# A new written order for a fused attention and feed-forward kernel, planned with re-measured transfer times and freer PSUM banks

## The chip, the cores and the metric

The kernel runs on one core of a Trainium2 chip. The metric is the device time of one execution in microseconds (us). Engines are named as in the profile: PE (matrix multiply), PEld (its weight loads), DVE (vector), ACT (scalar), POOL (GpSimd) and SP, whose only work here is to issue the DMA transfers.

## What is computed

```python
q_pool = q.reshape(B, H, S // 2, 2, D).mean(axis=3)          # B 4, H 8, S 1152, D 64
scores = np.matmul(q_pool, k.transpose(0, 1, 3, 2)) / np.sqrt(D)
scores = scores - np.max(scores, axis=-1, keepdims=True)
attn = np.exp(scores)
attn = attn / (np.sum(attn, axis=-1, keepdims=True) + 1e-09)
x = np.matmul(attn, v)        # then heads side by side: 2304 tokens x 512
h = x @ w_in                  # 512 x 2048
g = np.maximum(0.01 * h, h)
out = g @ w_out               # 2048 x 512
```

The two weight matrices come as 64-bit floats, everything else as 32-bit floats.

## The kernel before

There are 32 heads and then a feed-forward part of nine blocks of 256 tokens (`NB`), which begins as soon as the heads of a batch are finished, so that heads and blocks share the engines for most of the time.

**One head** (`hd`) is a chain of steps. Each step is a small function: `load_k`, `load_q`, `load_v` issue transfers; `k_tr` and `q_tr` transpose on PE, `k_hi`, `k_lo`, `q_hi`, `q_lo` split the results into a high and a low part on ACT and DVE; `q_dup` copies the parts to the other 64 partitions by DMA; six `qk` steps on PE (L453, L456) make scores only for their row maxima, which `vmax` takes on DVE (L468) and `vneg` combines; `m_tr`, `m_cp` and `m_dma` (L488) bring the maxima into rows; nine `qkt` steps (L503) make the scores again, transposed and with the maxima subtracted, `exp` (L507) takes the exponential on ACT, `esum` (L517) adds the tiles on POOL, `pv` (L529) multiplies with v. Then comes the tail of the head: `r_mm` (L540, L545) sums over partitions, `r_cp` copies to SBUF on ACT, `r_fold` (L563) issues four tiny transfers (two from head 12 on), `r_inv` (L568, L569) takes the reciprocal on DVE, `r_row` and `r_wide` send it to DRAM and back to 64 partitions, `norm` copies the pv result out of PSUM, `scale` (L583) multiplies on POOL, and `x_out` (L589) writes the head to DRAM.

**The weights** go through `w_load`, `w_f32` (ACT, then two DVE steps L614 and L617 that build 32-bit floats from the bits), `w_hi`, `w_lo` (L629, POOL) and `w_out_dma`. In the feed-forward part `l1` (L682) multiplies with w_in, and `l2` (L814 to L816) or `l2s` (L773) with w_out.

**The order.** All instructions of an engine are issued in the order in which the program writes them, and an instruction that waits holds up everything behind it on its engine; SP's transfers are such a queue too. The order is the string `ORDER`: one letter for each of 3557 steps, the letter names the family and the steps of a family come in a fixed sequence. `Scheduler.run` goes through it. For each step it looks up when its inputs and its buffer will be free in a model of the engines, and picks by it the buffer, the PSUM banks and, where a step may run on two engines, the engine. So the model's numbers do not change the letters, but they decide slots and engines. The letters themselves were found by a search with the same model outside of the kernel. In the model a transfer step of `n` DMAs takes 0.5 us of SP for each, and lands 1.2 us after its bytes have passed at 300 KB/us:

```python
if s.lat:                                                     # Scheduler.start
    end = self.dma = max(self.dma, end + 0.45) + s.lat
    end += 1.2
```

A DVE step marked `lock` waits in the model until POOL is free, and POOL waits until such a step has ended (`at`).

**PSUM** has eight banks. The two pairs (0, 1) and (2, 3) hold the score tiles of `qkt` (kind `s`) and the pairs (4, 5) and (6, 7) hold the tiles of `k_tr`, `q_tr`, `qk` and `m_tr` (kind `tp`); `r_mm` uses bank 6 (kind `t`) and `pv` bank 7 (kind `o`).

Of the kernel before, what the change touches and what calls it, by code (L numbers as in the profile page):

```python
# [24 lines left out]
LAT = 0.12  # L25
PELAT = 0.28
# [19 lines left out]
    "!#$%()!*+,,+#$++%-,,.--().*++.,,-.-.@-BB(A-../.01-.)!!*+A,-.23C+,-3-.4433-44.3.4./(#350$A143%B4#-33$B.%24-3434"  # L46
    ".&&&-.344-)3A*554555.+B,+3(3CB,6CC-4C4C.AA6-5553../7408123!!3)DDDE44EF-.6BB*++EF(&,9GG,:6F-.384-334.G-5-343.A-"
    ".../443;4#3$%031-B7A9.-H-.443-4.55!2.33-4.)34-43.*4.++5535(/<)0,,D=31#6>$D:;7A%CEEB4-6.4A-.9555!C2?B8<34=3-43("
    ".-3443H.-.&3-434*43../++#55$>,:,3F&F6%40157G9D#E$A;D%6-4)?38GD.H4H-.3:4-2343-.4-33..-5555434.3<.*/(=>!E+,+,B?6"
# [26 lines left out]
    "STV_`V_UVVUVVVVUUUUbVVVVVVa^bb^^V`VVVV_aUVVUUVbVVVVV_``daacbccbccUb^^VVVV^UbUVVVVV__^bUUVVV`^VVVccUVUVc_abVVV^"
    "_VV_`ab``a__aV^UUVVVVVVUUVVVb`a^UUUVVVVdddVVVVVVUUVV_bUb`abb`a^^ccVVVbbc_cb`a_``aa^_VVVVVVb^__`UUb`bVaV`VVVacc"
    "cV^ba_`abbbbbbbbbbbbbcdcccccdccbbcddd"
# [991 lines left out]
```

## Time and profile before

| | |
|---|---|
| median of 3 runs | 935.74 us (935.18 to 937.49) |
| the profiled execution, its own time | 939.89 us |
| its span, first to last instruction | 938.1 us |
| PE busy | 877.3 us, 94% of the span |
| DVE, POOL, ACT busy | 519.5, 485.3, 402.5 us |
| mean granted TensorE clock | 0.974 |

The profile comes from one execution. The busy time of an engine is the union of its instructions; idle time before an instruction is put down to what released it last. A busy PE can be at either level of its clock, which the rows show beside the busy time (1.00 is 2.4 GHz, 0.50 is 1.2 GHz). "SPq" rows are DMA issues on SP: their length is the time SP spent on issuing, not the transfer.

### The profile page before, as it was taken

How to read it: one execution, taken by the hardware profiler on the slowest of the kernel's cores; microseconds unless marked ns; L12 is line 12 of the kernel's file. 1: busy time of each engine (PE TensorE's matmuls, PEld its weight loads, DVE VectorE, ACT ScalarE, POOL GpSimd, SP SyncE). 2: the span in 40 equal slices, each digit the busy share in tenths (PEclk: the TensorE clock that was granted, in tenths of full speed). 3: DMA queues.
4: the chain of work that ended last, by engine and by line, in shares of the span. 5: the costliest groups of instructions: out<-in, count | busy, mean ns of one | idle time of the engine just before them, and what ended most of it. 6: DMA issues, size and time to landing. Idle time of an engine off the chain costs nothing.

```text
span 938.1 us, 19689 instructions
## 1 busy us (share of the span) xinstructions
PE 877.3 (94%) x7736; PEld 704.5 (75%) x7736; DVE 519.5 (55%) x806; ACT 402.5 (43%) x727; POOL 485.3 (52%) x386
## 2 busy tenths in 40 slices
PE   4989878889897999999999999999999999999997
PEld 2766546566685878777777776777779999999997
DVE  6677756656676763244446154444419974553353
ACT  2655455544455434433444534533442433422231
POOL 1656555558765769476757956955582101112000
PEclk9999998998898999999999999999999999999999
DMA  5565456466667555435545465264338777467651
GB/s 153 179 185 140 152 170 186 122 182 188 192 208 259 189 165 193 126 109 148 187 125 166 118 202 152 56 178 159 118 95 257 237 220 259 161 223 232 196 180 46
DMA packets 107309, 159.74 MB, mean 170 GB/s; under 512 B 25856, under 2 KB 74304, under 8 KB 107216
## 3 DMA queue, kind: packets, MB, share of 16 engines
q1 hardware_dynamic: 107216, 158.48, 54.8%
q8 instruction: 61, 1.00, 0.4%
q14 instruction: 32, 0.26, 0.1%
HBM read 131.12 MB, written 17.90 MB: 159 GB/s over the span
## 4 chain that ended last, share of the span: by engine, by line
PE 72%; DMA 9%; DVE 7%; SPq 4%; issue 2%; POOL 2%; ACT 2%; DVEq 0%; ACTq 0%; POOLq 0%
PE banks L682 21%; PE banks L503 13%; PE banks L529 12%; PE banks L773 10%; PE banks L453 4%; PE banks L814 3%; DVE stat L468 3%; PE banks L816 2%; PE banks L815 2%; DVE raw L614 2%; DMA rt<-rs 1%; DMA kn<-in_k_dram 1%; PE banks L540 1%; SPq L563 1%; DMA rs<-rd 1%
## 5 line engine op out<-in xcount | busy, mean ns | idle before, releaser
L468 DVE TENSOR_REDUCE stat<-banks 128x1 f32<-128x1024 f32 (+3 forms) x224 | 218.8, 1007 | 144.9 <-PE banks L453 118.6
L507 ACT ACTIVATE e<-banks 128x576 f32<-128x576 f32 x232 | 147.2, 649 | 127.1 <-PE banks L503 113.9
L517 POOL TENSOR_TENSOR sm<-sm,e 128x576 f32<-128x576 f32 x116 | 164.2, 1435 | 9.7 <-ACT e L507 8.5
L682 PE MATMUL banks<-xb,ws 128*128 128x256 f32 x1152 | 156.9, 290 | 0.4 <-issue 0.4
L682 PEld LDWEIGHTS banks<-xb,ws 128*128 128x128 f32 x1152 | 146.4, 193 | 10.3 <-issue 6.9
L503 PE MATMUL banks<-qh,ka 64*128 64x288 f32 x1152 | 147.3, 330 | 2.5 <-ACT e L507 1.2
L529 PE MATMUL banks<-e,vv 128*64 128x288 f32 x928 | 137.8, 411 | 1.2 <-DVE ql L424 1.1
L503 PEld LDWEIGHTS banks<-qh,ka 64*128 64x128 f32 x1152 | 103.0, 198 | 36.1 <-issue 13.2
L453 PE MATMUL banks<-ka,qh 64*128 64x512 f32 (+1 forms) x320 | 81.7, 486 | 33.3 <-DVE stat L468 15.7
L529 PEld LDWEIGHTS banks<-e,vv 128*64 128x64 f32 x928 | 69.4, 136 | 49.7 <-issue 5.4
L503 PE MATMUL banks<-mt,hot 64*128 64x288 f32 x576 | 92.6, 303 | 3.7 <-DMA mt<-ms 3.6
L503 PE MATMUL banks<-ql,ka 64*128 64x288 f32 x576 | 91.7, 304 | 0.0
L583 POOL TENSOR_TENSOR x<-x,rs 128x288 f32<-128x288 f32 x32 | 26.4, 827 | 101.9 <-DMA rs<-rd 88.5
L453 PEld LDWEIGHTS banks<-ka,qh 64*128 64x128 f32 (+1 forms) x320 | 33.6, 195 | 58.0 <-DVE stat L468 19.6
L682 PE MATMUL banks<-ka,ws 128*128 128x256 f32 x576 | 72.5, 282 | 1.4 <-DMA ws<-wd 1.4
L682 PEld LDWEIGHTS banks<-ka,ws 128*128 128x128 f32 x576 | 70.3, 188 | 2.5 <-issue 1.8
L517 POOL TENSOR_TENSOR sm<-e 128x576 f32<-128x576 f32 x32 | 47.1, 1473 | 35.4 <-ACT e L507 30.4
L503 PEld LDWEIGHTS banks<-mt,hot 64*128 64x128 f32 x576 | 60.7, 196 | 4.8 <-DMA mt<-ms 4.8
L773 PE MATMUL banks<-wo,gg 128*128 128x256 f32 x360 | 62.6, 282 | 0.3 <-DVE gg L749 0.3
L403 POOL TENSOR_TENSOR qs<-qn 112x384 f32<-112x384 f32 x32 | 33.2, 1036 | 52.5 <-DMA qn<-in_q_dram 33.9
L503 PEld LDWEIGHTS banks<-ql,ka 64*128 64x128 f32 x576 | 60.1, 196 | 0.0
L695 POOL TENSOR_TENSOR gg<-g,gg 128x512 fp32r<-128x512 f32 x32 | 41.7, 1305 | 26.3 <-ACT gg L248 15.9
(201 smaller groups left out, 1445.3 us busy)
## 6 DMA issues: line engine op xcount, KB each, us to landing
ws<-wd SPq DMA_DIRECT2D x144, 512.0 KB
kn<-in_k_dram SPq DMA_DIRECT2D x32, 288.0 KB
qn<-in_q_dram SPq DMA_DIRECT2D x128, 72.0 KB
vv<-in_v_dram SPq DMA_DIRECT2D x32, 288.0 KB
raw<-in_moe_w_in_dram SPq DMA_DIRECT2D x16, 512.0 KB
raw<-in_moe_w_out_dram SPq DMA_DIRECT2D x16, 512.0 KB
wd<-ws SPq DMA_DIRECT2D x16, 512.0 KB
rs<-rd SPq DMA_DIRECT2D x64, 72.0 KB
```

The costliest lines, as they stand in the source:

```text
L403: ENG[e].tensor_tensor(out=qs[hd][:n], in0=a, in1=b, op=ALU.add)
L453: nc.tensor.matmul(p[:n, x, :KW], lhsT=qh[hd][r, o:o + n], rhs=kh[r, :KW], start=True, stop=True)
L468: nc.vector.tensor_reduce(out=d, in_=p, axis=AX.X, op=ALU.max)
L503: nc.tensor.matmul(p[:, x, :HW], lhsT=w[r], rhs=m[r, hf * HW:(hf + 1) * HW], start=(n == 0), stop=(n == 3))
L507: nc.scalar.activation(out=ex[hd, u], in_=sps.pop((hd, u))[:, :, :HW], func=AF.Exp)
L517: ENG[e].tensor_tensor(out=o, in0=a, in1=b, op=ALU.add)
L529: nc.tensor.matmul(p[64 * hf:64 * hf + 64, :HW], lhsT=vv[hd][:, t, :], rhs=probs(hd, t, hf), start=(t == 0), stop=(t == KT - 1),)
L583: ENG[e].tensor_tensor(out=x1s[hd], in0=x1s[hd], in1=rss.pop(hd), op=ALU.mult)
L682: nc.tensor.matmul(p, lhsT=wst[i, f][:, a, c, :], rhs=xx[i][x][:, c, :], start=(n == 0), stop=(n == 3 * KC - 1))
L695: ENG[e].tensor_tensor(out=t[:, 1], in0=gf.pop((i, fp)), in1=f32(t[:, 0]), op=ALU.subtract)
L773: nc.tensor.matmul(o, lhsT=g[i, p][:, a], rhs=w[:, x], start=(p == 0 and n == 0 and half == 0), stop=(p == FH - 1 and n == 2), skip_group_ ...
L814: nc.tensor.matmul(p, lhsT=gh, rhs=wo[f][:, 0], start=(f == hf * FH), stop=False)
```

## The change

The change replaces the string `ORDER`. It also gives the model of `Scheduler` other numbers for transfers and a limit of ten transfers under way (`FLIGHTS`), and lets three kinds of PSUM tiles lie in more banks. No step, shape or instruction form is added or removed. The diff, with the string cut to one of its lines:

```diff
+FLIGHTS = 10
 ORDER = (
-    "!#$%()!*+,,+#$++%-,,.--().*++.,,-.-.@-BB(A-../.01-.)!!*+A,-.23C+,-3-.4433-44.3.4./(#350$A143%B4#-33$B.%24-3434"
...
+    "()*+,++!+,,,!@B(B)#$--%#$.-..*--..-.+.!+,B/0(%)1A-*+,.+B-!.-CCCC2.,3A-34,--.4.34#3../&&3$40A453-(1#%-..B4A3$53"
...
     def at(self, s, e, t):
         t = max(t, self.free[e])
+        if s.lat:
+            n, each = s.lat[0], s.eng["SP"] / s.lat[0]
+            for j in range(n):
+                i = len(self.flights) + j - FLIGHTS
+                t = max(t, self.flights[i] - j * each) if 0 <= i < len(self.flights) else t
+            return t
...
         if s.lat:
-            end = self.dma = max(self.dma, end + 0.45) + s.lat
-            end += 1.2
+            end = self.dma = max(self.dma, end + 0.6) + s.lat[1]
+            end += 0.45
+            self.flights += [end] * s.lat[0]
...
-    tags["tp"] = [(None, 0, slots("bank", (4, 5), (6, 7)))]
-    tags["t"] = [(None, 0, slots("bank", (6,)))]
-    tags["o"] = [(None, 0, slots("bank", (7,)))]
+    tags["tp"] = [(None, 0, slots("bank", (4, 5), (6, 7), (0, 1), (2, 3)))]
+    tags["t"] = [(None, 0, slots("bank", (6,), (7,)))]
+    tags["o"] = [(None, 0, slots("bank", (7,), (6,)))]
...
-    def sp(n, nbytes, run=512):
-        return dict(eng={"SP": 0.5 * n}, lat=nbytes / 300e3 * max(1.0, 512 / run))
+    def sp(n, nbytes, each=0.46, rate=250e3):
+        return dict(eng={"SP": each * n}, lat=(n, nbytes / rate))
```

Each transfer step gets its own `each`: 0.47 for `load_q` (rate 200e3), 0.58 for `q_dup` and `r_wide` (there 120e3), 0.78 for `m_dma`, 0.62 for `r_fold`, 0.41 for `r_row`, 0.6 for `x_out`, 0.5 for the weights, 0.36 for `ws_load`. Lines of the kernel after the change are 8 higher than before (L563 is L571).

In the program that results, 62 of the 288 `tp` tiles lie in banks 0 to 3, 39 of them in heads 0 to 13; five `pv` tiles lie in bank 6 and five `r_mm` tiles in bank 7. `norm` stands on DVE in 17 heads (before in 7), the copy of `post` in 13 of 32 (before in 8). Matmuls of the same tiling of the array follow each other in groups; PE goes from one tiling to another 265 times, before 290 times.

**SP around `r_fold` of heads 4 and 5** (`rt` is the target of `r_fold`, `mt` of `m_dma`, `rd` of `r_row`, `rs` of `r_wide`). Before:

```order
L387 DMA qn_70<-in_q_dram 48x3x128 x4
L589 DMA xd_74<-x_1286 64x288 x2
L433 DMA qh<-qh 64x288 x2
L600 DMA raw<-in_moe_w_out_dram 128x512
L433 DMA ql<-ql 64x288 x2
L563 DMA rt<-rs 48x1x6 x8
L488 DMA mt_73<-ms 1x5x128 x2
L572 DMA rd_82<-rt 96x6
```

After:

```order
L571 DMA rt<-rs 48x1x6 x4
L608 DMA raw<-in_moe_w_in_dram 128x4x128
L447 DMA vv<-in_v_dram 128x576
L366 DMA kn<-in_k_dram 128x576
L367 DMA kn<-in_k_dram 128x64
L496 DMA mt_73<-ms 1x5x128 x2
L580 DMA rd_82<-rt 96x6
L366 DMA kn<-in_k_dram 128x576
L367 DMA kn<-in_k_dram 128x64
L608 DMA raw<-in_moe_w_in_dram 128x4x128
L441 DMA ql<-ql 64x288 x2
L584 DMA rs<-rd_82 64x288 x2
```

The eight transfers of the two heads stood together, ahead of `m_dma` of head 7; now those of head 4 stand alone, and those of head 5 follow behind the last row shown.

**DVE around `r_inv` of the same heads** (`stat_66` and `stat_67` are the maxima of even and odd heads, here 8 and 7 or 9). Before:

```order
L471 TENSOR_REDUCE neg_69<-stat_67 128x5
L468 TENSOR_REDUCE stat_66<-banks 128x1 x2
L568 TENSOR_REDUCE rt<-rt 96x6
L569 RECIPROCAL rt<-rt 96x6
L568 TENSOR_REDUCE rt<-rt 96x6
L569 RECIPROCAL rt<-rt 96x6
L468 TENSOR_REDUCE stat_66<-banks 128x1
L379 TENSOR_TENSOR ka<-banks,ka 128x2x5x64
L468 TENSOR_REDUCE stat_66<-banks 128x1
```

After:

```order
L479 TENSOR_REDUCE neg_69<-stat_67 128x5
L576 TENSOR_REDUCE rt<-rt 96x6
L577 RECIPROCAL rt<-rt 96x6
L622 TENSOR_SCALAR raw<-raw 128x512 x2
L476 TENSOR_REDUCE stat_66<-banks 128x1 x3
L387 TENSOR_TENSOR ka<-banks,ka 128x2x5x64
L476 TENSOR_REDUCE stat_66<-banks 64x1
L476 TENSOR_REDUCE stat_66<-banks 128x4
L476 TENSOR_REDUCE stat_66<-banks 64x1
L479 TENSOR_REDUCE neg_68<-stat_66 128x5
L432 SCALAR_TENSOR_TENSOR ql<-banks,qh 64x288
L576 TENSOR_REDUCE rt<-rt 96x6
```

Both reciprocals stood between the second and the third maximum of head 8; now that of head 5 stands behind all maxima of head 8.

**PE at the start.** Before:

```order
L367 MATMUL banks<-ident,kn 128x64 x10
L412 MATMUL banks<-ident,qs 128x48 x6
L367 MATMUL banks<-ident,kn 128x64 x10
L453 MATMUL banks<-ka,qh 128x512 x6
L412 MATMUL banks<-ident,qs 128x48 x6
L453 MATMUL banks<-ka,qh 128x512 x2
```

After:

```order
L420 MATMUL banks<-ident,qs 128x48 x6
L375 MATMUL banks<-ident,kn 128x64 x10
L461 MATMUL banks<-ka,qh 128x512 x4
L375 MATMUL banks<-ident,kn 128x64 x10
L461 MATMUL banks<-ka,qh 128x512 x2
L420 MATMUL banks<-ident,qs 128x48 x6
```

The transposes of q come first (on SP the transfers of q stand ahead of those of k), and two `qk` steps of head 0 stand ahead of `k_tr` of head 1.

## Rows read from the trace of the kernel before

**Rows 1.** The page, busy time by engine and granted clock by fortieth.

```profile
PE 877.3 (94%) x7736; PEld 704.5 (75%) x7736; DVE 519.5 (55%) x806; ACT 402.5 (43%) x727; POOL 485.3 (52%) x386
...
PEclk9999998998898999999999999999999999999999
```

**Rows 2.** Busy time by stretch: start:end, length, engines (instructions), clock, DMA share, GB/s.

```profile
0.00:30.00 30.00, 16.26 (x117) 11.15 (x119) 19.90 (x30) 9.30 (x17) 5.40 (x14) 1.00 0.58 164
30.00:305.00 275.00, 239.73 (x2340) 171.53 (x2338) 184.35 (x231) 146.51 (x273) 169.92 (x131) 0.91 0.59 180
305.00:705.00 400.00, 396.23 (x3446) 300.30 (x3445) 179.11 (x240) 170.36 (x318) 281.89 (x216) 1.00 0.49 147
705.00:938.10 233.10, 225.04 (x1847) 221.54 (x1843) 136.13 (x308) 76.33 (x120) 28.09 (x28) 1.00 0.61 200
```

**Rows 3.** PE's waits, 30 to 305: sum in us, times, longest.

```profile
PE banks L453 <- DVE stat L468: 12.9, 6, 5.4
PE banks L453 <- DMA qh<-qh: 5.2, 4, 2.3
PE banks L453 <- DVE ka L379: 4.1, 3, 3.6
PE banks L503 <- DMA mt<-ms: 3.6, 4, 1.5
PE banks L453 <- ACT x L248: 3.3, 2, 2.3
```

**Rows 4.** All engines' waits, 30 to 305: `norm` on ACT.

```profile
ACT x L248 <- DMA xd<-x: 17.5, 6, 4.5
```

**Rows 5.** Instructions in time, DVE and PE: start, length, what, [idle before <-releaser].

```profile
139.60 0.16 DVE L568 TENSOR_REDUCE rt<-rt 96x6 f32<-96x12 f32 x1 [3.83 <-DMA rt<-rs]
...
142.83 0.79 PE L453 MATMUL banks<-ka,qh 64*128 64x512 f32 x2 [5.44 <-DVE stat L468]
```

**Rows 6.** Instructions in time, SP's issues at the same place.

```profile
134.05 5.92 SPq L563 DMA_DIRECT2D rt<-rs  x8
```

**Rows 7.** Instructions in time, DVE at 96 and DVE, POOL and PE from 285.

```profile
96.01 3.90 DVE L614 TENSOR_SCALAR raw<-raw 128x512 uint32<-128x512 uint32 x1
...
286.70 7.97 DVE L614 TENSOR_SCALAR raw<-raw 128x512 uint32<-128x512 uint32 x1 [2.90 <-ACT raw L611]
...
285.07 5.53 POOL L517 TENSOR_TENSOR sm<-sm,e 128x576 f32<-128x576 f32 x4
290.55 2.49 POOL L629 TENSOR_TENSOR ws<-raw,ws 128x512 fp32r<-128x512 f32 x2
...
295.86 0.80 PE L453 MATMUL banks<-ka,qh 64*128 64x512 f32 x2 [5.18 <-DVE stat L468]
```

**Rows 8.** Sum over the nine stretches between 63 and 302 with clock 0.50.

```profile
sum 47.60, PE 44.75 PEld 37.48 DVE 26.75 ACT 19.18 POOL 22.00; mean PE 4.97 PEld 4.16 DVE 2.97 ACT 2.13 POOL 2.44
```

**Rows 9.** Instructions in time, PE from one tiling to another.

```profile
309.12 0.40 PE L815 MATMUL banks<-wo,gg 128*128 128x512 f32 x1
309.36 0.40 PE L816 MATMUL banks<-wo,gg 128*128 128x512 f32 x1
309.69 0.27 PE L477 MATMUL banks<-ident,neg 64*128 64x64 f32 x2
```

**Rows 10.** One line's instructions, SP's issues: min/median/max ns, first and last start.

```profile
L563 SPq DMA_DIRECT2D rt<-rs x88: 501/584/1812, 55.2 to 712.4; - x88
...
L488 SPq DMA_DIRECT2D mt<-ms x64: 691/739/837, 20.9 to 684.0; - x64
```

**Rows 11.** Instructions in time at the start.

```profile
2.12 1.87 SPq L387 DMA_DIRECT2D qn<-in_q_dram  x4
...
10.92 0.79 PE L453 MATMUL banks<-ka,qh 64*128 64x512 f32 x2 [2.65 <-DVE ka L379]
```

**Rows 12.** Groups by line, DVE 30 to 305 and the page: busy, mean ns of one.

```profile
L468 DVE TENSOR_REDUCE stat<-banks 128x1 f32<-128x1024 f32 x56 | 67.3, 1220 | 39.6 <-PE banks L453 34.8 <-ACT x L248 4.4
...
L507 ACT ACTIVATE e<-banks 128x576 f32<-128x576 f32 x232 | 147.2, 649 | 127.1 <-PE banks L503 113.9
```

More of the change, by code (lines that the diff above doesn't have):

```diff
@@ L76 @@
[L76 to L78 removed]
+    "()*+,++!+,,,!@B(B)#$--%#$.-..*--..-.+.!+,B/0(%)1A-*+,.+B-!.-CCCC2.,3A-34,--.4.34#3../&&3$40A453-(1#%-..B4A3$53"
+    "43)-244355BB%-43!4.3.4(*+3,53+6,-A.443-../7433B45)0631A4DDD9-E8(EE*6.-!4+,2+),-..BCCF#BCCA$:6%3CF(-34;8-..433!"
@@ L79 @@
+    "`^_a`a`abbbdddcbbbbccbbbbbcccbbbccddd"
 )
@@ L111, in __init__, with add @@
         self.steps, self.after, self.holds, self.dma = {}, {}, {}, 0.0
-        self.done, self.log, self.locked, self.tiled = set(), [], 0.0, 0
-    def add(self, key, run, eng, lat=0.0, deps=(), order=(), takes=(), lock=False):
+        self.done, self.log, self.locked, self.tiled, self.flights = set(), [], 0.0, 0, []
+    def add(self, key, run, eng, lat=None, deps=(), order=(), takes=(), lock=False):
         assert key not in self.steps, key
@@ L854, in pool, with step @@
         return {"POOL": gp(n), "DVE": dve(n) + OND} if kind in ON_DVE else {"POOL": gp(n)}
-    def step(fn, *a, eng, lat=0.0, deps=(), order=(), takes=(), lock=False):
+    def step(fn, *a, eng, lat=None, deps=(), order=(), takes=(), lock=False):
         sch.add((fn.__name__, *a), partial(fn, *a), eng, lat, [d for d in deps if d], [d for d in order if d], takes, lock)
@@ L878, in tile_pooled_attention_moe @@
         step(load_v, hd, **sp(1, 0.3e6), order=after("load_v"), takes=[("vv", [("pv", hd, NBU - 1)])])
-        step(load_q, hd, **sp(4, 0.3e6), order=after("load_q"), takes=[("qn", [("q_sum", hd)])])
+        step(load_q, hd, **sp(4, 0.3e6, 0.47, 200e3), order=after("load_q"), takes=[("qn", [("q_sum", hd)])])
         step(q_sum, hd, eng=pool(QT * D, "q_sum"), lock=True, deps=[("load_q", hd)], order=after("q_sum"), takes=[("qs", [("q_tr", hd)])])
@@ L891, in tile_pooled_attention_moe @@
         if hd >= NEAR:
-            step(q_dup, hd, 0, **sp(2, 0.15e6), deps=high)
-            step(q_dup, hd, 1, **sp(2, 0.15e6), deps=low)
+            step(q_dup, hd, 0, **sp(2, 0.15e6, 0.58), deps=high)
+            step(q_dup, hd, 1, **sp(2, 0.15e6, 0.58), deps=low)
             high, low = [("q_dup", hd, 0)], [("q_dup", hd, 1)]
@@ L904, in tile_pooled_attention_moe @@
         step(m_cp, hd, eng={"ACT": act(128, True)}, deps=[("m_tr", hd)], takes=[("ms", [("m_dma", hd)])])
-        step(m_dma, hd, **sp(2, 0.01e6), deps=[("m_cp", hd)] + ([("zeros", hd)] if 0 < hd < len(mts) else []), takes=[("mt", [last])])
+        step(m_dma, hd, **sp(2, 0.01e6, 0.78), deps=[("m_cp", hd)] + ([("zeros", hd)] if 0 < hd < len(mts) else []), takes=[("mt", [last])])
         ready = [("k_lo", hd)] + high + low + [("m_dma", hd)]
@@ L930, in tile_pooled_attention_moe @@
                 step(r_cp, hd, eng={"ACT": act(HW, True)}, deps=[("r_mm", hd)], takes=[("rs", [("scale", hd)])])
-                step(r_fold, hd, **sp(2 * parts(hd), 0.002e6), deps=[("r_cp", hd)], takes=[("rt", [("r_row", hd)])])
+                step(r_fold, hd, **sp(2 * parts(hd), 0.002e6, 0.62), deps=[("r_cp", hd)], takes=[("rt", [("r_row", hd)])])
                 step(r_inv, hd, eng={"DVE": 0.38 if parts(hd) == 2 else 0.2}, deps=[("r_fold", hd)])
-                step(r_row, hd, **sp(1, 0.002e6), deps=[("r_inv", hd)])
-                step(r_wide, hd, **sp(2, 0.15e6), deps=[("r_row", hd)])
+                step(r_row, hd, **sp(1, 0.002e6, 0.41), deps=[("r_inv", hd)])
+                step(r_wide, hd, **sp(2, 0.15e6, 0.58, 120e3), deps=[("r_row", hd)])
                 step(scale, hd, eng=pool(HW, "scale"), lock=True, deps=[("r_wide", hd), ("norm", hd)])
-                step(x_out, hd, **sp(2, 0.15e6), deps=[("scale", hd)])
+                step(x_out, hd, **sp(2, 0.15e6, 0.6), deps=[("scale", hd)])
     seq = [o * NF + g * FH + i for g in range(2) for o in range(2) for i in range(FH)]
@@ L941, in tile_pooled_attention_moe @@
         half, at = divmod(i % NF, FH)
-        step(w_load, i, **sp(1, 0.524e6), order=[("w_load", seq[n - 1])] if n else [], deps=([("w_f32", i - NF, 2)] if o else []))
+        step(w_load, i, **sp(1, 0.524e6, 0.5), order=[("w_load", seq[n - 1])] if n else [], deps=([("w_f32", i - NF, 2)] if o else []))
         step(w_f32, i, 0, eng={"ACT": act(512)}, deps=[("w_load", i)])
@@ L948, in tile_pooled_attention_moe @@
         if not o:
-            step(w_out_dma, i, **sp(1, 0.524e6), deps=[("w_lo", i)])
+            step(w_out_dma, i, **sp(1, 0.524e6, 0.5), deps=[("w_lo", i)])
     for p in range(FH):
```

61 lines of the change are left out of this document (31 added, 30 removed).

## The prediction

> **What bounds the kernel now.** I read the page first: PE is busy for 94% of the span, no other engine for more than 55%, so only PE's own time counts, and the question is where PE stands still or runs at its low clock [rows 1]. The page's clock line has its 8s and 9s between the third and the thirteenth fortieth, and none after. The table by stretch makes this sharp [rows 2]. In the first 30 us PE is busy for 16.3: start-up. From 30 to 305 it is idle for 275.0 - 239.7 = 35.3 us, at a mean clock of 0.91. From 305 to 705 it is idle for 3.8 of 400, and in the last 233 us for 8.1. So a new order can win little behind 305; there it can only keep what is there.
>
> The low clock has its own sum: nine stretches, 47.6 us together, with PE busy in them for 44.8 [rows 8]. At 1.2 instead of 2.4 GHz half of that, 22.4 us, is lost. Each of these stretches begins within a few microseconds of a PE wait, so I let this loss go with the waits. Together 35.3 + 22.4 = 57.7 us between 30 and 305 stand open, and that is the room that the change has.
>
> Next, what ends PE's waits there [rows 3]. Five groups make 29.1 of the 35.3 us. Two name transfers: `q_dup` (5.2 us) and `m_dma` (3.6). One names `norm` on ACT (3.3 us), and ACT stood for `x_out`'s transfer, 17.5 us in all [rows 4], so this is a transfer too. Two name DVE (12.9 and 4.1 us), and the sequence in time tells why DVE was late. The longest, 5.4 us at 142.8: DVE had `r_inv` in front of a maximum, and its input landed only at 139.6; the eight tiny issues of `r_fold` alone took SP 5.9 us [rows 5, 6]. The second, 5.2 us at 295.9: DVE's L614 took 7.97 us, for POOL went through six of its steps without a break [rows 7]. The 4.1 us are the same kind: L614 at 96.0 took 3.90. So by cause: transfers that are late in front of an in-order engine, 5.2 + 3.6 + 3.3 + 5.4 = 17.5 us; L614 behind POOL, with what is left of the DVE groups, 12.9 - 5.4 + 4.1 = 11.6 us; the remaining 6.2 are many short waits.
>
> **The change part by part.** It adds and removes no instruction, so the sum has only moved work in it.
>
> *Transfers.* The old model charges 0.5 us of SP for each DMA; the trace has 0.74 for `m_dma` and 0.58 (longest 1.81) for `r_fold` [rows 10], and the new numbers are 0.78 and 0.62. So the old order thought SP ahead of where it was, and put consumers too early; the new one should not. At the place of the longest wait the excerpts show it: the eight issues are pulled apart, and `r_inv` of head 5 stands behind five more maxima. I take that wait (5.4 us) as gone. Of the other transfer waits, 12.1 us, I take a quarter, 3.0, because the steps that wait are still in the same queues, and a new order brings new misses. Together 8.4. Bounds: all 17.5 gone, or none, since a wait can come back at another place.
>
> *L614 behind POOL.* The pile-up on POOL comes from `scale` waiting for `r_wide`, then `esum` following without a break. Better transfer times make this rarer, but the model's rule for the two engines is the same in both, so I take a third: 3.9 us. Bounds 0 and 11.6. The row first: 7.97 us [rows 7] is far longer than one POOL step, 5.53 / 4 = 1.4 us. The Trainium skill, "SBUF — State Buffer", section "SBUF: two separate sides", says that VectorE and GpSimd share a pair of ports as an exclusive lock, which whoever starts first keeps for a whole instruction. Read as one instruction's wait, it would cap each such delay at 1.4 us, and this term would be near 0, the sum 6.4 us smaller (with its share of the clock). The row shows a DVE instruction passed over several times in a row, so I keep the term.
>
> *The clock.* 8.4 + 3.9 = 12.3 us of 35.3 idle go, 35%; of the 22.4 us of low clock the same share, 7.8. Bounds 0 and 22.4.
>
> *Fewer changes of tiling.* At a change the next matmul starts 0.33 us after the last, without one 0.24 [rows 9]: about 0.1 us. 25 fewer make 2.5 us, all on PE, wherever PE is the bound, which is nearly everywhere. Bounds 1 and 2.5.
>
> *The start.* PE stood 2.65 us at 10.9 for `k_lo` of head 1, which held a PSUM pair; with pairs (0, 1) and (2, 3) open and `qk` ahead of the second `k_tr` this goes. Against it q's transfers, 1.87 us of issuing, stand ahead of k's [rows 11]. Two of the four q halves also no longer stand between DVE's first maxima. I take a gain of 1.5; bounds -1.9 (a loss) and 2.7.
>
> *Behind 305.* PE idles so little there (3.8 us [rows 2]) that another order can hardly gain. I charge 2 us for new short waits; bounds 0 and 8, twice what is there.
>
> *PSUM banks.* 62 `tp` tiles now take a pair that the `qkt` tiles need. Their readers are DVE's maxima, 1.22 us, instead of an `exp`, 0.65 [rows 12]. In the order most of them are followed by a `pv` (over 2 us of PE work) or `l1` steps before the pair is used again, which covers 0.57 us, so I cost it at nothing; without that cover it is the rival below. *DVE instead of ACT* for ten `norm` and five `post` steps: about 0.45 us each on DVE, which is busy for 184 of 275 us [rows 2]: hidden, unless DVE is just then behind.
>
> Sum: 8.4 + 3.9 + 7.8 + 2.5 + 1.5 - 2.0 = 22.1 us less. It is made against the profiled execution, 939.89 us of its own time with a span of 938.1; its span would be 916. The median of the runs is 935.74, 4.2 below that execution; the same 22.1 from the median gives 913.6, and I say **914 us**.
>
> **The rivals.**
>
> *All early transfer waits go.* If the new transfer times are right nearly everywhere, 17.5 + 11.6 = 29.1 us of waits go, with 82% of the clock's loss, 18.5; with 2.5 and 1.5 the gain is 51.6, the time 884. For it: the longest waits are all of these two kinds. Against it: four in-order queues between 30 and 305 are at work, three of them busy for more than half of the time (DVE 184, POOL 170, ACT 147 of 275 us [rows 2]), so some collision is always there. Half way to it, 899, is where I draw the line to the forecast.
>
> *The waits only move.* SP issues about as many transfers per head as before, 22, and the weights besides. If SP's queue itself sets the pace up to 305, a better model cannot shorten it; waits of the same length stand at other places. Then only 2.5 + 1.5 - 2.0 = 2.0 us are left: 934. For it: eight issues took 5.9 us [rows 6]. Against it: those eight stood together only by the order, which now parts them, and L614's 7.97 us are no matter of SP.
>
> *Slower: score tiles blocked by maxima.* If a `tp` tile in banks 0 to 3 holds up the next `qkt`, each costs 1.22 - 0.65 = 0.57 us of PE, 62 of them 35 us. That eats the 22 us and leaves 13 more: 949. It decides from 22.1 / 62 = 0.36 us per tile on. For it: DVE is the engine that is late [rows 3], and when L614 stands, `qkt` would now stand too, where it could go on before. Against it: the covering work named above, and 39 of the 62 tiles lie in the stretch where PE has gaps anyway.
>
> **How the numbers follow.** About 0.3% (2.8 us) is what a measurement can tell from no change here; faster means below 932.9, slower above 938.5. The forecast, a gain of 6 to 37 us, has 0.60. Nearly all waits gone: 0.14. Waits only move: 0.12, of which 0.09 fall within 0.3% and the rest just below it. Slower: 0.14. So faster 0.77, same 0.09, slower 0.14. The range goes from 894 (with the upper bounds of transfers and half of the lock term) to 940, where the third rival is held and the fourth begins; beyond lie some 0.09 below and 0.11 above. The likeliest case's own range is 899 to 930.
>
> **What would show it.** In the profile after: PE idle between 30 and about 290 of 23 us instead of 35, fewer or shorter stretches at 0.50 (about 30 us in all instead of 47.6), no PE wait of over 3 us behind `r_inv`, `r_fold` rows of four, at least one L614 still over 3 us, the stretch of 400 us behind it as tight as before, and the first `qk` before 10 us. Wrong it would be if the 47.6 us stay, or if `exp` or `qkt` wait for DVE's maxima in sum for over 10 us.

## The result and the profile after

The changed kernel takes 899.28 us (median of 4 runs, 897.51 to 902.16) against 935.77 for the kernel before: a ratio of 0.961, 95% interval 0.9581 to 0.9639, or 36.5 us less. The forecast was 914, so the direction and the range held, and the gain was larger than the 22 us of the sum. The profiled execution took 897.51 us with a span of 895.7; against that of before (939.89) it is 42.4 us shorter, some 6 more than between the medians, since the profiled run of before lay 4.2 above its median and this one 1.8 below. The clock has a part in that: the profiled execution of before has a mean granted clock of 0.974, where 61 executions of the same kernel beside the experiments have 0.972 to 0.985, with a median of 0.979; the four of the changed kernel have 0.988 to 0.991. The terms below add up to the 42.4.

Lines of the changed kernel stand eight further down: L453 is L461 now, L468 L476, L503 L511, L614 L622, L617 L625.

The page of the kernel after: PE's busy time, and the granted clock in 40 slices. Against [rows 1] the row of 9s has one 8 where there were four.

```profile
PE 861.3 (96%) x7736; PEld 693.0 (77%) x7736; DVE 524.2 (59%) x813; ACT 390.4 (44%) x706; POOL 494.3 (55%) x400
...
PEclk9999899999999999999999999999999999999999
```

Busy time by stretch; the columns are those of [rows 2]. The bound at 665 is the same place in the work as 705 was before (PE has started 5894 and 5903 matmuls by then); at 300, where the dense stretch ends now, the changed kernel is 220 matmuls further than the old one was at 305.

```profile
0.00:30.00 30.00, 18.04 (x140) 13.14 (x142) 20.53 (x33) 12.88 (x24) 7.17 (x15) 1.00 0.68 205
30.00:300.00 270.00, 253.90 (x2537) 182.70 (x2533) 187.94 (x252) 156.93 (x291) 190.25 (x146) 0.96 0.65 195
300.00:665.00 365.00, 363.21 (x3217) 274.65 (x3215) 184.36 (x257) 148.64 (x283) 258.37 (x198) 1.00 0.50 149
665.00:895.70 230.70, 226.14 (x1856) 222.46 (x1852) 131.31 (x273) 72.00 (x110) 38.50 (x43) 1.00 0.62 202
```

PE is idle for 16.1 us in the second stretch, where it was 35.3; for 1.8 in the third (3.8) and 4.6 in the last (8.1). The stretches at low clock, which were nine and 47.60 us [rows 8], are now five:

```profile
sum 20.40, PE 18.41 PEld 15.16 DVE 14.66 ACT 9.67 POOL 11.07; mean PE 3.68 PEld 3.03 DVE 2.93 ACT 1.93 POOL 2.21
```

Half of 18.41 is lost at 1.2 GHz, 9.2 us, where it was 22.4. PE's waits from 30 to 300 in the kernel after, sum, times, longest:

```profile
PE banks L511 <- DVE stat L476: 3.7, 3, 3.0
PE banks L464 <- ACT x L256: 3.0, 1, 3.0
PE banks L511 <- DMA mt<-ms: 1.9, 2, 1.4
PE banks L420 <- DVE stat L476: 1.7, 1, 1.7
PE banks L485 <- DVE neg L479: 1.3, 2, 1.1
PE banks L461 <- ACT x L256: 1.2, 1, 1.2
```

Against [rows 3] the 12.9 us of `qk` (L461) behind maxima are gone from the head of the list, as are the 5.2 us behind `q_dup` and the 4.1 behind `k_lo`. What is left of transfers is `mt`, 1.9, and twice `norm` on ACT (`x`, L256), 3.0 + 1.2, where ACT stood for `x_out`: 6.1 us in all instead of 17.5. What is left with DVE is 3.7 + 1.7 + 1.3 and two small ones (`k_lo` 0.5, maxima 0.3): 7.5 us. The 11.6 of the prediction is not its counterpart, for it left out the small DVE groups of before, 3.8 us, which the prediction put with the short waits; counted alike, DVE's part was 15.4. The first of these groups is new in kind: it is `qkt` (L511) that waits for maxima.

SP's own waits tell what the new order did to the queue. From 30 to 305, the two longest groups in the kernel before, both of `m_dma`:

```profile
SPq L488 <- ACT ms L481: 8.4, 3, 4.8
SPq L488 <- ACT e L507: 6.8, 3, 5.0
```

and in the kernel after the longest, and the longest of `m_dma` (L674 is `ws_load`, L496 `m_dma`):

```profile
SPq L674 <- DMA wd<-ws: 7.2, 2, 5.1
...
SPq L496 <- ACT ms L489: 5.2, 4, 2.4
```

SP stands little less, 65 us in all groups where it was 70, but at other steps. Ahead of `m_dma`, whose data a `qkt` needs soon, it stood for 19.1 us in 14 waits, the longest 5.0; now for 14.7 in 16, the longest 2.4. The longest group now is `ws_load`, the weights.

One of the two longest waits of the kernel after (2.96 us; the other, 3.03, is that of `norm` above), in time. DVE had three L625 from 101.78 on, the first and the third at the usual 0.69. The second took 4.23 us, from 102.39 to 106.62: a POOL step was under way when it began, and two more ran before it ended. The maxima followed at 107.25, and `qkt` stood for them:

```profile
101.78 1.57 POOL L411 TENSOR_TENSOR qs<-qn 112x384 f32<-112x384 f32 x1 [3.24 <-DMA qn<-in_q_dram]
101.78 5.44 DVE L625 SCALAR_TENSOR_TENSOR raw<-raw 128x512 uint32<-128x512 uint32 x3
...
103.31 1.40 POOL L525 TENSOR_TENSOR sm<-e 128x576 f32<-128x576 f32 x1
...
104.67 1.40 POOL L525 TENSOR_TENSOR sm<-e,gg 128x576 f32<-128x576 f32 x1
...
107.25 2.36 DVE L476 TENSOR_REDUCE stat<-banks 128x1 f32<-128x1024 f32 x2
...
108.53 0.84 PE L511 MATMUL banks<-qh,ka 64*128 64x288 f32 x4 [2.96 <-DVE stat L476]
```

Two more of PE's waits stand behind an L625 that took four times the usual 0.69:

```profile
67.58 2.83 DVE L625 SCALAR_TENSOR_TENSOR raw<-raw 128x512 uint32<-128x512 uint32 x1
...
71.31 0.28 PE L485 MATMUL banks<-ident,neg 64*128 64x64 f32 x2 [1.10 <-DVE neg L479]
...
262.14 2.85 DVE L625 SCALAR_TENSOR_TENSOR raw<-raw 128x512 uint32<-128x512 uint32 x1
...
266.27 0.39 PE L420 MATMUL banks<-ident,qs 48*128 48x48 f32 x6 [1.73 <-DVE stat L476]
```

So 2.96 + 1.10 + 1.73 = 5.8 of the 7.5 us with DVE are still of the kind "DVE behind POOL". All 32 instructions of each of the two lines (min/median/max ns, first and last start):

```profile
L622 DVE TENSOR_SCALAR raw<-raw x32: 381/427/1651, 41.5 to 298.9; 128x512 uint32<-128x512 uint32 x32
L625 DVE SCALAR_TENSOR_TENSOR raw<-raw x32: 659/693/4234, 42.5 to 299.8; 128x512 uint32<-128x512 uint32 x32
```

L622, which had the 7.97 of [rows 7], has 1.65 at most; the pile-up is at L625, the part of `w_f32` that follows it, and half as long.

### The profile page after: what moved, and what is told of

The parts are those of the page before. It is cut to its first block, busy times and chain, and to the rows that moved or that the text cites. A ratio compares the mean times of both kernels' runs of the same rounds, so it can differ in the third digit from the quotient of the medians.

```text
span 895.7 us, 19761 instructions
## 1 busy us (share of the span) xinstructions
PE 861.3 (96%) x7736; PEld 693.0 (77%) x7736; DVE 524.2 (59%) x813; ACT 390.4 (44%) x706; POOL 494.3 (55%) x400
## 4 chain that ended last, share of the span: by engine, by line
PE 81%; DMA 6%; DVE 6%; SPq 2%; issue 2%; ACT 2%; POOL 0%; DVEq 0%; ACTq 0%; POOLq 0%
PE banks L690 22%; PE banks L511 17%; PE banks L537 13%; PE banks L781 11%; PE banks L461 4%; PE banks L822 3%; PE banks L824 3%; PE banks L823 3%; DVE stat L476 2%; DMA rt<-rs 2%; PE banks L553 1%; DMA ws<-wd 1%; DMA raw<-in_moe_w_in_dram 1%; PE banks L548 1%; SPq L571 1%
## 5 line engine op out<-in xcount | busy, mean ns | idle before, releaser
L476 DVE TENSOR_REDUCE stat<-banks 128x1 f32<-128x1024 f32 (+3 forms) x224 | 217.6, 1005 | 113.5 <-PE banks L461 96.7
L690 PE MATMUL banks<-xb,ws 128*128 128x256 f32 x1344 | 176.4, 285 | 0.3 <-DMA ws<-wd 0.2
L690 PEld LDWEIGHTS banks<-xb,ws 128*128 128x128 f32 x1344 | 167.4, 190 | 10.2 <-issue 4.8
L525 POOL TENSOR_TENSOR sm<-sm,e 128x576 f32<-128x576 f32 x119 | 171.0, 1454 | 3.4 <-ACT e L515 2.0
L511 PE MATMUL banks<-qh,ka 64*128 64x288 f32 x1152 | 146.5, 330 | 5.9 <-DVE stat L476 4.0
L511 PEld LDWEIGHTS banks<-qh,ka 64*128 64x128 f32 x1152 | 93.9, 191 | 52.6 <-issue 18.6
L511 PE MATMUL banks<-mt,hot 64*128 64x288 f32 x576 | 89.8, 297 | 2.2 <-DMA mt<-ms 2.2
L511 PE MATMUL banks<-ql,ka 64*128 64x288 f32 x576 | 88.1, 296 | 0.0
L461 PE MATMUL banks<-ka,qh 64*128 64x512 f32 (+1 forms) x320 | 69.4, 445 | 6.4 <-ACT ka L256 2.2
L511 PEld LDWEIGHTS banks<-mt,hot 64*128 64x128 f32 x576 | 58.1, 189 | 3.3 <-DMA mt<-ms 3.1
L511 PEld LDWEIGHTS banks<-ql,ka 64*128 64x128 f32 x576 | 57.3, 190 | 0.0
L432 DVE SCALAR_TENSOR_TENSOR ql<-banks,qh 64x288 fp32r<-64x288 f32 x66 | 29.9, 453 | 46.1 <-ACT qh L429 45.3
L703 POOL TENSOR_TENSOR gg<-g,gg 128x512 fp32r<-128x512 f32 x32 | 41.8, 1311 | 22.1 <-DVE gg L256 11.6
L822 PE MATMUL banks<-wo,gg 128*128 128x512 f32 x128 | 53.3, 416 | 0.0
L824 PE MATMUL banks<-wo,gg 128*128 128x512 f32 x128 | 50.9, 398 | 0.0
```

Source lines behind the costliest of these rows:

```text
L461: nc.tensor.matmul(p[:n, x, :KW], lhsT=qh[hd][r, o:o + n], rhs=kh[r, :KW], start=True, stop=True)
L476: nc.vector.tensor_reduce(out=d, in_=p, axis=AX.X, op=ALU.max)
L511: nc.tensor.matmul(p[:, x, :HW], lhsT=w[r], rhs=m[r, hf * HW:(hf + 1) * HW], start=(n == 0), stop=(n == 3))
L525: ENG[e].tensor_tensor(out=o, in0=a, in1=b, op=ALU.add)
L690: nc.tensor.matmul(p, lhsT=wst[i, f][:, a, c, :], rhs=xx[i][x][:, c, :], start=(n == 0), stop=(n == 3 * KC - 1))
L703: ENG[e].tensor_tensor(out=t[:, 1], in0=gf.pop((i, fp)), in1=f32(t[:, 0]), op=ALU.subtract)
```

## The experiments

Two readings of the gain were open after this. **Misplaced steps**: a few steps stood too early in their queue, each cost its wait and the low clock behind it, and each can be had back alone. **Pace of the queues**: what is late is a queue, so a wait that is taken away comes back a little later. A third is that the **PSUM banks**, not the order, made the gain. In the experiments the engine and the buffers of every step are written out as planned, so that an edit moves only what it names; names are `step(head, part)`, and for weights `w_f32(weight, part)`. Lines stand 190 higher there than in the kernel that was edited (in the kernel before L453 becomes L643, `qk`; L468 L658, `vmax`; L477 L667, `m_tr`; the copy of `norm` L438; `q_dup` L623; `r_fold` L753). Each run is set against executions of the kernel before beside it, and the range behind a ratio is its 95% interval.

### r_inv alone

The kernel before, `r_inv` of heads 4 and 5 later on DVE, `r_row` and `r_wide` later on SP, `scale(4)` next to `scale(5)`:

```diff
- DVE: vmax(8,1) r_inv(4) r_inv(5) vmax(8,2) ... vneg(8) vmax(9,0)
+ DVE: vmax(8,1) vmax(8,2) ... vneg(8) r_inv(4) r_inv(5) vmax(9,0)
  SP:  r_fold(4) r_fold(5) m_dma(7)
```

> The kernel before, with r_inv of heads 4 and 5 (and the steps that need them) written behind the maxima of head 8; r_fold's eight issues on SP stay where they are, ahead of m_dma of head 7. Misplaced steps: the 5.4 us wait at 142.8 goes, but m_dma of head 7 is now the late one, since it is issued behind the eight; a qkt wait for mt of 2 to 5 us takes its place, and the gain is 1 to 3 us. Pace of the queues: the wait only moves, gain under 1. If r_inv's place alone was the cause: 5.4 us and the 3.4 us that the 6.8 us of low clock behind it cost, a gain of 8 to 9.

Measured: 941.86 us against 936.14, ratio 1.0065 (1.0028 to 1.0102): slower. PE's waits of over 2 us from 130 to 160:

```profile
137.41 0.37 PE L667 MATMUL banks<-ident,neg 64*128 64x64 f32 x2 [3.35 <-DVE stat L658]
...
155.16 0.79 PE L643 MATMUL banks<-ka,qh 64*128 64x512 f32 x1 [2.70 <-DMA qh<-qh]
...
159.14 0.79 PE L643 MATMUL banks<-ka,qh 64*128 64x512 f32 x1 [2.22 <-ACT x L438]
```

The 5.44 us of [rows 5] are gone, and 8.3 us stand in their place. The wait for `mt` that I had named is not among them; a transpose behind DVE, a `q_dup` and a `norm` are. No theory had it slower.

### r_fold later as well

The same, and the two `r_fold`, eight issues, behind `m_dma`:

```diff
- SP:  q_dup(8,1) r_fold(4) r_fold(5) m_dma(7)
+ SP:  q_dup(8,1) m_dma(7) r_fold(4) r_fold(5)
```

> As the run with r_inv later, and r_fold of heads 4 and 5 behind m_dma of head 7 on SP. Misplaced steps: no PE wait over 2 us near 143 and no low clock there; gain 5.4 + 3.4 = 8.8 us, between 6 and 10. Pace of the queues: other transfers are late in their place, gain under 2. PSUM banks as the change's main part: nothing to gain by order, 0 to 2.

Measured: 938.04 against 936.14, ratio 1.0024 (0.9992 to 1.0056): no gain. Four rows tell why, two of PE and two of SP's issues:

```profile
148.68 0.50 PE L643 MATMUL banks<-ka,qh 64*128 64x512 f32 x1
...
155.97 0.79 PE L643 MATMUL banks<-ka,qh 64*128 64x512 f32 x1 [6.79 <-DMA qh<-qh]
...
137.28 5.54 SPq L753 DMA_DIRECT2D rt<-rs  x8
...
153.33 1.17 SPq L623 DMA_DIRECT2D qh<-qh  x2
```

and the same places in the kernel before:

```profile
155.63 0.50 PE L453 MATMUL banks<-ka,qh 64*128 64x512 f32 x2
...
151.39 1.17 SPq L433 DMA_DIRECT2D qh<-qh  x2
```

The first `qk` of head 9 starts 7 us earlier than before (148.68 instead of 155.63); the second one needs `q_dup`, which SP issues at 153.33 instead of 151.39, and PE stands for 6.79. The first `qk` of head 10 starts at 172.82, and started at 171.28 before. So the wait was handed on within one head, to the next transfer in the same queue.

### The two r_fold parted

As the change has it: four issues before `m_dma`, four behind `q_dup` of head 9, and what follows from each later.

```diff
- SP:  r_fold(4) r_fold(5) m_dma(7) ... r_wide(5) q_dup(9,0) x_out(4)
+ SP:  r_fold(4) m_dma(7) ... r_wide(4) load_v(8) q_dup(9,0) r_fold(5) x_out(4) ... r_row(5) w_load(10) r_wide(5)
- DVE: vmax(8,1) r_inv(4) r_inv(5) vmax(8,2) ... vmax(9,2) w_f32(18,1)
+ DVE: vmax(8,1) vmax(8,2) k_lo(9) vmax(8,3) r_inv(4) ... vmax(9,2) r_inv(5) w_f32(18,1)
- POOL: scale(5) w_lo(7) ... w_lo(17)
+ POOL: w_lo(7) ... w_lo(17) scale(5)
```

> The kernel before, with the two r_fold parted as the change parts them: r_fold of head 4 and its four issues stay, m_dma of head 7 follows at once, r_fold of head 5 stands behind q_dup of head 9, and r_inv, r_row, r_wide and scale of both heads are each written later. It was seen that moving the eight issues as a block only handed the wait on, to a q_dup behind it on SP (6.8 us at 156). Misplaced steps, now read as one block of eight issues: four at a time delay nobody over 2 us; the 5.4 us go with 3.4 us of low clock, gain 6 to 9, no PE wait over 2.5 between 130 and 165. Pace of SP's queue: the second four or r_wide hold up another transfer, a wait of 4 us or more comes back within 30 us, gain under 2.

Measured: 940.6 against 937.67, ratio 1.0019 (0.9992 to 1.0046): no gain again. Now ACT is the place: its `norm` stands 7.85 us for an `x_out` that came later, and PE stands for it, and again 20 us on.

```profile
156.30 0.40 ACT L438 COPY x<-banks 128x288 f32<-128x288 f32 x1 [7.85 <-DMA xd<-x]
...
156.75 0.79 PE L643 MATMUL banks<-ka,qh 64*128 64x512 f32 x1 [3.73 <-ACT x L438]
...
171.97 0.43 PE L646 MATMUL banks<-ka,qh 64*128 64x128 f32 x4 [2.57 <-ACT x L438]
...
176.48 0.79 PE L643 MATMUL banks<-ka,qh 64*128 64x512 f32 x1 [2.78 <-DMA qh<-qh]
```

Here, in the middle of the dense stretch, the reading of misplaced steps falls three times.

### L614 later

```diff
- DVE: w_f32(24,1) vmax(15,0) vmax(15,1) vmax(15,2) vmax(15,3)
+ DVE: vmax(15,0) vmax(15,1) vmax(15,2) w_f32(24,1) vmax(15,3)
```

> The kernel before, with the step w_f32 of weight 24, part 1 (the L614 of 7.97 us at 286.7) written behind the maximum 2 of head 15 on DVE. Misplaced steps: the 5.2 us wait at 295.9 goes, and 3.4 us with it for 6.8 us of low clock; gain 8.6, between 6 and 10. Pace of DVE and POOL: L614 or the next lock step is held as long a few us later, and PE waits there; gain under 2.

Measured: 929.31 against 936.14, ratio 0.991 (0.9874 to 0.9946): 7 to 8 us from one step (5 to 12 by the interval), as expected. The L614 (L804 here) takes 1.67 us instead of the 7.97 of [rows 7], and PE's 5.18 us are gone: it is idle for 30.0 us from 30 to 305 instead of 35.3. The 6.8 us of low clock at 295 are gone too. Ahead of 286, where the two kernels issue the same, the low clock is 31 us here and was 41 before, and that is no doing of the step:

```profile
30.00:305.00 275.00, 245.00 (x2410) 174.51 (x2407) 188.50 (x243) 152.84 (x285) 177.55 (x137) 0.94 0.62 187
...
288.72 1.67 DVE L804 TENSOR_SCALAR raw<-raw 128x512 uint32<-128x512 uint32 x1
```

Why this one stays gained and the others not is not shown by a run. My reading is that behind it PE is the bound by itself, with 3.8 us idle in 400 [rows 2], so that no queue is late there that could take the wait over.

### Both together

> Both edits in one kernel: r_inv and r_fold later, and w_f32 later. Misplaced steps: the gains add, 8.8 + 8.6 = 17.4, between 13 and 19, so half of what the whole change gains comes from 14 steps. Pace of the queues: under 4. The two places lie 150 us apart, so a sum that is off by more than 2 would say that a delay is handed on.

Measured: 933.08 against 936.14, ratio 0.9966 (0.9938 to 0.9993): 3 us less. The sum of the two medians would be 4.9 less; within the intervals that is the same, and far from 17.

### The banks alone

The kernel before in its own order, 31 `tp` tiles in other pairs, among them:

```diff
- k_tr(1): banks 4, 5;  qk(0,0): 4, 5;  qk(5,1): 4, 5;  k_tr(7): 4, 5
+ k_tr(1): banks 0, 1;  qk(0,0): 2, 3;  qk(5,1): 2, 3;  k_tr(7): 0, 1
```

> The kernel before in its own order; only 31 of the tp tiles (qk, k_tr, q_tr, m_tr) up to head 14 lie in another pair of banks, wherever a pair had been given back earlier in the written order: 24 of them in banks 0 to 3. PSUM banks as the change's main part: the waits of qk for DVE's maxima (12.9 us) and for k_lo (4.1 us) shrink, gain 6 to 15. Order and transfers as the main part: 1 to 3 us at the start (2.65 us at 10.9 goes), nothing elsewhere but 0 to 2. Score tiles blocked by maxima: up to 24 times 0.57 = 14 us slower.

Measured: 940.65 against 937.67, ratio 1.0039 (1.0015 to 1.0063): 3 to 4 us slower. PE's waits from 30 to 305, the groups that speak of it (L643 is `qk`, L693 `qkt`):

```profile
PE banks L643 <- DVE stat L658: 10.5, 7, 4.7
PE banks L693 <- DVE stat L658: 8.5, 7, 2.0
...
PE banks L693 <- DVE ka L569: 4.0, 1, 4.0
```

`qk` waits for maxima 10.5 instead of 12.9 us, but `qkt` now waits for them, 8.5 us in seven waits, and `k_lo`'s 4 us moved from `qk` to `qkt`. That is the mechanism of my rival with blocked score tiles; its price was up to 14 us for these tiles, and the whole run is 3 to 4 slower. The start gained as foreseen: PE is busy for 17.50 of the first 30 us instead of 16.26. So the banks alone are not the gain. Whether the new order would do without them was not tried.

One more thing stands in this run. PE is idle for 275.00 - 232.56 = 42.4 us between 30 and 305, more than before, yet its low clock is shorter: six stretches, 27.30 us, instead of 47.60. This sets one execution against one: the two profiled ones have mean clocks of 0.984 and 0.974, and the ten of this kernel (0.975 to 0.984) and the 19 of before beside them (0.972 to 0.983) lie nearly alike. So the banks are not shown to change the low clock; the same order can give very different amounts of it. The stretch by itself, then the sum over the six:

```profile
30.00:305.00 275.00, 232.56 (x2331) 165.46 (x2328) 186.92 (x233) 145.13 (x271) 169.79 (x131) 0.95 0.60 181
```

```profile
sum 27.30, PE 24.68 PEld 22.96 DVE 16.28 ACT 11.35 POOL 3.80; mean PE 4.11 PEld 3.83 DVE 2.71 ACT 1.89 POOL 0.63
```

### One place of the change undone

The changed kernel with the block of eight issues back:

```diff
- SP:  r_fold(4) w_load(8) load_v(6) load_k(10) m_dma(7) ... r_wide(4) r_fold(5)
+ SP:  r_fold(4) r_fold(5) w_load(8) load_v(6) load_k(10) m_dma(7) ... r_wide(4)
- DVE: vmax(8,1) vmax(8,2) ... vneg(8) q_lo(9,0,0) r_inv(5)
+ DVE: vmax(8,1) r_inv(5) vmax(8,2) ... vneg(8) q_lo(9,0,0)
```

> The changed kernel with one part undone: r_fold of head 5 behind r_fold of head 4 again (eight issues), and r_inv of head 5 ahead of the maximum 2 of head 8. Misplaced steps: the wait of before comes back, 3 to 6 us of PE idle behind r_inv and 2 to 4 us of low clock; 5 to 9 us slower than the changed kernel's 899.3, so 904 to 908. Pace of the queues: under 2 us slower, since the same eight issues were on SP anyway.

Measured: 906.42 us, 0.9653 of before (0.9613 to 0.9693). That is 7.1 us over the changed kernel by the medians and 4 by the ratios, whose intervals overlap, so the loss is not clear of noise. In the profiled executions PE is idle for 21.7 us from 30 to 305, in the changed kernel for 16.1, and one of the new waits is at this place:

```profile
30.00:305.00 275.00, 253.25 (x2502) 181.56 (x2502) 184.76 (x249) 155.10 (x287) 188.41 (x144) 0.94 0.65 192
...
119.56 7.83 SPq L761 DMA_DIRECT2D rt<-rs  x8
...
131.77 1.50 SPq L686 DMA_DIRECT2D mt<-ms  x2
...
133.82 1.13 PE L701 MATMUL banks<-mt,hot 64*128 64x288 f32 x2 [2.79 <-DMA mt<-ms]
```

The eight issues hold `m_dma` back (SP issues it at 131.77, in the changed kernel at 124.95), and PE stands 2.8 us for `mt`; behind `r_inv`, where 3 to 6 us were expected, it stands 1.0 us at 130. So the eight in a row seem to cost something where the rest is on time, while parting them gives nothing where the rest is late.

### Which queue carries the gain

Three kernels in which one or two queues follow the other kernel's order up to step 1,350 (about the end of head 14) and the rest is left. SP of the changed kernel undone, an excerpt:

```diff
- SP:  q_dup(8,0) w_load(23) r_fold(4) w_load(8) load_v(6) load_k(10) m_dma(7) r_row(4)
+ SP:  q_dup(8,0) w_load(22) q_dup(8,1) r_fold(4) r_fold(5) m_dma(7) r_row(4) w_load(23)
```

> The changed kernel with one queue undone: SP's steps among the first 1,350 stand in the relative order that they have in the kernel before, as far as dependencies and buffers let them (11 steps go earlier); PE, ACT, DVE and POOL keep the changed order. Transfers' order as the main part: 10 to 20 us slower than 899.3. Consumers' places on DVE, ACT and POOL as the main part: 0 to 5 slower. Only the fit of all queues counts: more than 15 slower, with long waits for transfers.

Its mirror, the old kernel with the new SP:

> The mirror of it: the kernel before, with SP's steps among the first 1,350 in the changed kernel's relative order (15 steps go earlier); the other four queues keep the old order. Transfers' order as the main part: 10 to 20 us faster than 936. Consumers' places as the main part: 0 to 5 faster. Only the fit of all queues counts: no gain, or slower.

And the changed kernel with the old DVE and POOL:

> The changed kernel with DVE's and POOL's steps among the first 1,350 in the relative order of the kernel before (17 steps go earlier); PE, ACT and SP keep the changed order. Transfers' order as the main part: 0 to 5 slower than 899.3. Places on DVE and POOL, L614 and L617 behind POOL among them, as the main part: 10 to 20 slower, with L622 of over 3 us back. Only the fit counts: more than 15 slower.

Measured: 999.78, 1023.88 and 1043.7 us, ratios to before of 1.0696 (1.066 to 1.0732), 1.094 (1.0907 to 1.0973) and 1.1154 (1.1122 to 1.1187). Every mixture is 64 to 108 us slower than the kernel before, which is the slower of the two that it is mixed from. From 30 to 330, old SP first, then new SP, then old DVE and POOL:

```profile
30.00:330.00 300.00, 224.48 (x2160) 158.22 (x2162) 158.37 (x214) 132.95 (x248) 152.36 (x118) 0.85 0.47 139
```

```profile
30.00:330.00 300.00, 216.03 (x2071) 148.61 (x2066) 160.69 (x209) 127.32 (x238) 152.56 (x118) 0.85 0.47 141
```

```profile
30.00:330.00 300.00, 206.70 (x1925) 141.93 (x1922) 147.93 (x193) 119.26 (x222) 133.43 (x104) 0.81 0.42 124
```

PE is idle for 76, 84 and 93 of 300 us. Neither SP's order nor DVE's and POOL's is worth anything without the rest (PE's and ACT's orders were not put back alone): with the old SP order, SP itself stands for `r_inv` that DVE now does later,

```profile
SPq L770 <- DVE rt L767: 24.0, 4, 9.3
```

and the transfers behind it in the queue wait with it. The mixtures answer which queue carries the gain (none of those tried); they don't split it.

They don't tell either why the new order is the better one. It came from a new search with other transfer times, a limit on transfers under way and freer banks, all at once. Orders searched with only one of these, or again with the old model, were not run, so it is open whether the re-measured times made the gain.

### Trying for more

The changed kernel with seven steps moved, each behind what waited for it:

```diff
- ACT: norm(4) exp(5,6)
+ ACT: exp(5,6) norm(4)
- ACT: norm(8) exp(9,6) exp(9,7)
+ ACT: exp(9,6) exp(9,7) norm(8)
- DVE: w_f32(7,2) w_f32(16,2) w_f32(17,2) vmax(7,0) vmax(7,1) vmax(7,2)
+ DVE: w_f32(7,2) vmax(7,0) vmax(7,1) vmax(7,2) w_f32(16,2) w_f32(17,2)
...
```

> The changed kernel with seven steps moved behind what waited for them: norm of head 8 behind exp 7 of head 9, norm of head 4 behind exp 6 of head 5, w_f32 part 2 of weights 16 and 17 behind maximum 2 of head 7, w_f32 part 2 of weight 24 behind vneg of head 15, vneg of head 4 ahead of w_f32 part 2 of weight 3, m_dma of head 7 ahead of load_v of head 6. Misplaced steps: the waits 3.0 + 3.0 + 1.2 + 1.4 + 1.7 + 1.1 = 11.4 us go for the greater part, and low clock with them: 6 to 12 us below 899.3, so 887 to 893. Pace of the queues, or waits handed on as in the runs with r_fold moved: 897 to 902.

Measured: 897.64 us, 0.9569 of before (0.9527 to 0.9612). Then five more, aimed at its three waits of over 2 us:

```diff
- DVE: r_inv(4) w_f32(18,1) w_f32(19,1) vmax(8,1)
+ DVE: vmax(8,1) r_inv(4) w_f32(18,1) w_f32(19,1)
- SP:  q_dup(10,1) r_row(7) x_out(6)
+ SP:  x_out(6) q_dup(10,1) r_row(7)
...
```

> The run with seven moves, and five more for the three waits that it still has over 2 us: r_inv of head 4 and w_f32 part 1 of weights 18 and 19 behind maximum 1 of head 8 (2.8 us at 126), w_f32 part 1 of weight 25 behind vneg of head 15 (2.4 us at 264), x_out of head 6 ahead of q_dup of head 10 on SP (2.4 us at 172). Misplaced steps: 4 to 7 us and the clock behind them go, 889 to 894. Waits handed on, as in the runs with r_fold moved: 896 to 902. The queues' fit broken: above 902.

Measured: 896.1 us, 0.9598 of before (0.9572 to 0.9624). The changed kernel's interval is 0.9581 to 0.9639: the second ratio lies in it, and the first lies just below it with an interval that overlaps it, so neither can be told from it. PE's busy time from 30 to 305 says the same; the profiled execution of the changed kernel has 258.90 there. First the seven moves, then the twelve:

```profile
30.00:305.00 275.00, 257.01 (x2555) 184.21 (x2556) 188.23 (x255) 158.28 (x293) 194.86 (x150) 0.98 0.65 194
```

```profile
30.00:305.00 275.00, 258.69 (x2571) 188.07 (x2568) 188.89 (x255) 159.37 (x294) 196.57 (x151) 0.97 0.65 194
```

PE's idle time is no shorter than the 16.1 us of the changed kernel (18.0 and 16.3), so the 11.4 us of waits that were aimed at came back in other places, as with `r_fold`.

## Why the prediction was right, and where it was not

The terms, in us gained between the two profiled executions:

| term | forecast | measured | from |
|---|---|---|---|
| transfers | 8.4 | 11.4 | 17.5 to 6.1 of PE's waits |
| L614 behind POOL, all DVE groups | 3.9 | 7.9 | 15.4 to 7.5 (the forecast had 11.6) |
| the other short waits | 0 | -0.1 | 2.4 to 2.5 (the forecast had 6.2) |
| clock | 7.8 | 13.2 | 22.4 to 9.2 |
| fewer changes of tiling | 2.5 | 2.7 | what is left of the 42.4 |
| start | 1.5 | 1.8 | PE busy 16.26 to 18.04 in the first 30 us |
| behind 305 | -2.0 | 5.5 | 11.8 to 6.4 idle |

**Right**: where the gain lies (32.4 of 42.4 us are idle time and low clock between 30 and 305), the direction, and the start. The range held, with the gain of 36.5 between the medians well above the 22.1 of the sum. The tiling's 2.7 is only what the other rows leave over, so nothing shows that term by itself.

**L614 behind POOL, too small**: I took a third of 11.6 us. All DVE groups together lost 7.9 of 15.4. Of that, the waits that were traced to a DVE step held by POOL went from 5.18 + 3.60 = 8.8 us to 5.8, so about a third of them did go; the larger part of what went, 6.6 to 1.7 us, is other waits for DVE, which I had left with the L614 sum or at nothing without looking for their cause.

**Transfers, mis-sized**: 8.4 was 5.4 + a quarter of the other 12.1, "because the steps that wait are still in the same queues, and a new order brings new misses". About half of them went, 12.1 to 6.1 us. The step "I take that wait (5.4 us) as gone" came true in the result, but as the price of that place it was wrong: taken away alone, in three ways, that wait is worth nothing, since another transfer or `norm` is late behind it. So where this term came near, it was partly luck. What fits the runs is that the 19 us of idle time belong to an order in which the queues fit each other, and that a sum of single places was the wrong model for them; which part of the new order does it was not found.

**The clock**: taken by share, 35% of 22.4. By shares the measured 54% of the idle time would give 12.2, and it was 13.2, so this term's miss follows from the idle time. Yet part of this size is the pick of the execution: the one profiled before had 0.974, the median of 61 others is 0.979. An estimate from the mean clocks, 2 x (1 - clock) x span, gives 39 us of low clock in such a typical execution of before and 19 in the changed kernel, and with PE busy in them as in the two profiles the term would be about 10. Nor is the share a law: the run with other banks had more idle time and 20 us less low clock.

**Behind 305, wrong sign**: I charged 2 us for new short waits, "another order can hardly gain". The stretch of 400 us held, 1.8 us idle in 365 where it was 3.8 in 400; most of the 5.5 comes from the last 231 us, 8.1 to 4.6, which I had read in the table and did not take as open. No run was made on this part. The change also moved work between engines there: 12 more of the sums and differences of L741 (L749 after) run on POOL, 28 instead of 16.

**The rivals**: "all early transfer waits go" has its edge at 899, and the median, 899.28, landed on it; its own 884 is not reached, for 13.6 us of waits with a cause are left. "Waits only move" was wrong for the change, and its outcome was right for every single move of `r_inv` and `r_fold`, and for the twelve moves at the end. "Score tiles blocked" exists, 8.5 us in the run with banks alone and 3.7 in the changed kernel, 2.96 of them behind the L625 above.

**What would show it**: I asked for no wait of over 3 us behind `r_inv`, low clock well under 47.6, rows of four for `r_fold`, the middle as tight and the first `qk` before 10 us. All came; that `qk`:

```profile
9.33 0.80 PE L461 MATMUL banks<-ka,qh 64*128 64x512 f32 x2 [2.22 <-ACT ka L256]
```

The statement that an L614 of over 3 us would remain was wrong by its line, and right for its neighbour L625, 4.23 us. The row at 101.78 also bears on the rule that I weighed in the prediction (the Trainium skill, "SBUF — State Buffer", section "SBUF: two separate sides"): the L625 of 4.23 us outlasted the POOL step under way and two that started after it, so that here too a wait of a single instruction, 1.57 us at most in these rows, would be too short.

## What to carry to other kernels

A wait in a trace is what a place costs, not what moving a step there gains: before pricing a moved step, look in the next head for the transfer or buffer that is late next, and count as gain only what PE keeps up to there. In this kernel the wait at the end of the dense stretch, with PE the bound behind it, could be had alone (7 us from one step); those tried in the middle could not, and the whole new order gained there. And queues that are written to fit each other are not to be mixed: one or two queues of another good order cost 64 us and more. Before a reading rests on one execution's low clock, compare the mean clocks of several.

## What had not been expected

That a single wait of 5.4 us could be taken away in three ways without any gain, and once at a loss of 6 us. That PE's low clock does not go by idle time: 42.4 us idle with 27.30 us of low clock in the run with other banks, 35.3 with 47.60 before, and 31 or 41 us of it in the same first 286 us of work; what sets it was not settled. And that a DVE step was held over three and more POOL steps in a row, in both orders (7.97 us and 4.23 us).
